# A fourth w_mod row in the last stage, its products on GpSimd, and gradient products and copies in another order

## The chip, the cores and the metric

One core of a Trainium2 chip runs the kernel. The metric is the device time of one execution in microseconds, the median over several runs. A core has five engines with a queue each: TensorE (PE, with its weight loads shown as PEld), VectorE (DVE), ScalarE (ACT), GpSimd (POOL) and SyncE (SP). DMAs are issued from the queues of SP, POOL and ACT.

## What is computed

The forward pass of one transformer-like block and all its gradients: an adaptive layer norm, a spectral filter (2D real FFT, a product with a complex weight, inverse FFT), a second adaptive layer norm and an MLP with GELU. All data is bf16, with 2048 tokens, D = 1024 and F = 3584.

```python
def _A_ref(x, w_r, w_i):
    X = rfft2(x.astype(float32), axes=(-2, -1)) * (w_r + 1j * w_i)
    return irfft2(X, s=(S, D), axes=(-2, -1)).astype(bfloat16)
def _B_ref(x, w1, b1, w2, b2):
    h = gelu(einsum('bsd,df->bsf', layernorm(x), w1) + b1)
    return einsum('bsf,fd->bsd', h, w2) + b2
mod = (silu(c) @ w_mod).reshape(1, 6, 1, -1)
sa, ca, ga, sb, cb, gb = (mod[:, k] for k in range(6))
h = layernorm(A_x) * (1 + ca) + sa
x = A_x + ga * _A_ref(h, A_w_r, A_w_i)
h = layernorm(x) * (1 + cb) + sb
out = x + gb * _B_ref(h, B_w1, B_b1, B_w2, B_b2)
# returned: out, and the gradients for A_x, A_w_r, A_w_i, B_w1, B_b1, B_w2, B_b2, c, w_mod
```

Three of the gradients matter here. The gradient of w_mod (1024 x 6144, out_9) is the outer product of silu(c) and the six gradient rows of mod, each 1024 long. The gradient of c (out_8) needs, for each of those rows, the product of w_mod with that row. The gradients of the MLP weights (out_6 for w2, out_4 for w1) are products over all 2048 tokens.

## The kernel before

The work is a single long program, with no loop left on the chip. The FFTs are matrix products with cosine and sine matrices, split by symmetry into four classes of 512 rows (CE, CO, SE, SO). The part that the change touches is the last third: the backward pass through the spectral filter, beside which the weight gradients of the MLP are computed.

**Filler products.** A generator, `pieces` (L1504), yields one weight gradient product at a time: 16 matmuls of 128x512 into one PSUM buffer, 56 products for out_6 (`gw2_product`) and then 56 for out_4 (L1550). `fill(n)` takes n products from it, so the places of the `fill` calls are where TensorE gets work beside the spectral steps. Four PSUM buffers (`ps_f`) serve the products, and a few of the spectral steps too. ScalarE copies each out_4 product to one of eight buffers in `gwo1` (L1554), and a store from there is issued on POOL's queue, or on SP's for the last three (L1556). The gradient of gelu's input, d_gz, comes in as transposing DMAs on SP (`gw1_load`, L1495), one pair per group of eight products.

**The pair stage.** `spectral_core` runs eight pairs of frequency blocks (`pair`); after each, `beside_bwd` (L1589) takes four products from `fill` and up to three steps of a ring, `gmod_ring` (L1185), that works on rows 3 and 4 of w_mod's gradient: 16 steps, one for each of the eight 128-row blocks of each row. A step reduces a block of w_mod against the gradient row (VectorE, L1201), forms the block of out_9 in the same buffer (VectorE, L1203), stores it (POOL's queue, L1204) and loads the block two steps on (SP's queue, L1190). The ring has three buffers, so a load waits for the store of an earlier step. The loads of the transposed activations for the out_6 products (hhsA, L1507 and L1509) are on SP's queue too.

**The split inverse.** After the pairs, `half_class` (L1422) forms V for the classes CO and SO, with two matmuls of half width, ScalarE evacuations (L807, by the helper `s_copy`) and VectorE sums. One product is filled in behind CO. Then four chunks of output follow (L775), and `consume_bwd` (L1460) finishes each: unfolding on VectorE, the backward pass of the layer norm (`scaled_rows`, `ln_bwd`), a column sum on TensorE (`halves_sum`, L218), and the store of out_1. `ln_bwd` reduces on VectorE (L1244), scales on ScalarE by the result (L1246) and adds on VectorE. In the first chunk and the third, products are filled in between the output blocks, and in all of them behind the store of out_1 and behind the column sum.

**The last stage.** When the chunks are done, rows 5, 2, 1 and 0 of w_mod's gradient follow (`gmod_row`, `gmod_steps`), each with six products behind it, and then the products that are left. A row is broadcast from DRAM into one of two `gr` buffers. Each of its eight steps loads a block of w_mod (SP's queue, L1176, four buffers), forms the block of out_9 in one of four buffers (VectorE, L1177), stores that (POOL's queue, L1178) and reduces on VectorE (L1179). The gradient of c is formed from all the reductions at the end.

**What sets the order.** A planner fixes each engine's order at build time. It takes the program's order as the priority and emits what its own estimates of durations call ready, so a product may come earlier or later than its `fill` call; copies out of PSUM have a raised priority. `issue_after(x)` makes each instruction that is traced in its block, on x's engine, stand behind x in that engine's queue; it is an order and not a wait. At run time each queue is worked off in order, with semaphores between the engines.

Of the kernel before, what the change touches and what calls it, by code (L numbers as in the profile page):

```python
# [13 lines left out]
ACT = mybir.ActivationFunctionType  # L14
ALU = mybir.AluOpType
# [20 lines left out]
def kernel(  # L36
# [24 lines left out]
    nc = tc.nc  # L61
    CE, CO, SE, SO = 0, 1, 2, 3
# [131 lines left out]
    def tt(out, a, b, op):  # L194
        return nc.vector.tensor_tensor(out=out, in0=a, in1=b, op=op)  # L195
# [188 lines left out]
    for j in range(4):  # L384
        for cch in range(NDC):
            pt = ps_f("pt")
            for a in range(4):
                q = (0, 2, 3, 1)[a] if j % 2 == 0 else (1, 3, 2, 0)[a]
# [159 lines left out]
    def spectral_core(fwd, fb, sms, em, css, pt, evac_u, evac_c, evac_v, consume, o4tag, pfs=None, fill=lambda n: None, mid=lambda: None, beside=lambda n, r_in: None):  # L548
# [156 lines left out]
        for par in range(2):  # L705
            for m in range(4):
# [14 lines left out]
                if par == 0 and m > 0:  # L721
# [6 lines left out]
                    else:  # L728
                        cl = (CE, SE)[m - 2]
# [4 lines left out]
        for cl in (CO, SO):  # L734
            if fwd:
                s_inv_half(cl, smis[1], 0)
                continue
            Vs[cl] = reg.tile([P, 8, 512], BF16, name=f"V{cl}", tag=f"uv{cl}")

            def r_cols(c8, i, cl=cl):  # L740
                dc = c8 // 2
                base = (0, 1, 2, 1)[dc] + 256 * (c8 % 2) + (PW if (dc >= 2) == (cl < 2) else 0)
                return R[:, cl * 4 + i, :, :].rearrange("p x w -> p (x w)")[:, base:base + 255:2]

            half_class(cl, Vs[cl], r_cols, evac_v)
            if cl == CO:
                fill(1)
        with tc.issue_after(r_in[0].ins):
            nc.vector.tensor_scalar(out=gm[:, 8:12, :], in0=gm[:, 4:8, :], scalar1=-1.0, scalar2=None, op0=ALU.mult)
        xts = [reg.tile([P, 4, D], BF16, name="xt", tag="sma")[:]]  # L750
# [6 lines left out]
        for i in range(4):  # L757
            if fwd and i == 0:
                tmp, eb, o4 = first
            else:  # L760
                o4, on, tmp = ct[:, 3 * (i % 2)], ct[:, 3 - 3 * (i % 2)], ct[:, 1 + i % 2]
                if fwd and i == 2:
                    eb = tmp
            half = [(cl, eb[:, 2 * k + cl // 2], k * 256 + i // 2 * P) for cl in (CE, SE) for k in range(2)]
            for npp, (cl, ov4, c0) in enumerate((half if i % 2 == 0 else []) + [(cl, o4[:, cl], i * P) for cl in (CO, SO)]):
                if npp in (2, 4):
                    fill(1)
                for hh_ in range(2):
                    npo[0] += 1
                    po = ((ps_d, ps_s) if fwd else (ps_d, ps_s, ps_d, ps_f))[npo[0] % (2 if fwd else 4)]("po")  # L770
                    for d2 in range(2):
                        dc = 2 * hh_ + d2
                        for h in range(2):
                            gi = 2 * dc + h + (4 if (dc >= 2 and cl >= 2) else 0)
                            nc.tensor.matmul(po[:, d2 * 256:(d2 + 1) * 256], lhsT=Vs[cl][:, 2 * dc + h, c0:c0 + P],  # L775
                                             rhs=gm[:, gi, :], start=(h == 0), stop=(h == 1))
                    with tc.high_priority():
                        ov = ov4[:, hh_ * 512:(hh_ + 1) * 512]
                        if fwd or (cl, hh_) != (3, 0):
                            nc.any.tensor_copy(out=ov, in_=po[:])  # L780
                        else:
                            last_po[0] = nc.scalar.copy(out=ov, in_=po[:])
            if i % 2 == 0:
                tt(o4[:, 0:4:2, :], eb[:, 0:2, :], eb[:, 2:4, :], ALU.add)
                if fwd and i == 2:
                    tt(on[:, 0:4:2, :], eb[:, 0:2, :], eb[:, 2:4, :], ALU.subtract)
            elif not fwd or i == 1:
                tt(o4[:, 0:4:2, :], eb[:, 0:2, :], eb[:, 2:4, :], ALU.subtract)
            if i == 0:
                if fwd:  # L790
                    for cl in (CO, SO):
                        s_inv_half(cl, smis[1], 1)
                    ct = reg.tile([P, 4, 4, D], BF16, name="ct", tag=o4tag)
                xts.append(reg.tile([P, 4, D], BF16, name="xt", tag="smb" if fwd else "px0")[:])
            consume(i, o4, tmp, ct[:, 2 - i % 2], xts[i % 2], eb)
# [376 lines left out]
    def gmod_steps(r, wrs, gws, gr):  # L1172
        nc.sync.dma_start(out=gr, in_=d_gmod[r * D:(r + 1) * D].partition_broadcast(P))
        for jc in range(NDC):
            wr, gw = wrs[:, jc % wrs.shape[1], :], gws[:, jc % gws.shape[1], :]
            nc.sync.dma_start(out=wr, in_=w_mod[jc * P:(jc + 1) * P, r * D:(r + 1) * D])  # L1176
            nc.vector.tensor_scalar(out=gw, in0=gr, scalar1=u_rt[:, jc:jc + 1], scalar2=None, op0=ALU.mult)  # L1177
            nc.gpsimd.dma_start(out=out_9[jc * P:(jc + 1) * P, r * D:(r + 1) * D], in_=gw)  # L1178
            nc.vector.tensor_tensor_reduce(out=wr, in0=wr, in1=gr, scale=1.0, scalar=0.0,  # L1179
                                           op0=ALU.mult, op1=ALU.add, accum_out=gu[:, r, jc:jc + 1])  # L1180
            yield
# [57 lines left out]
    def ln_sums(gs):  # L1239
        nc.vector.tensor_scalar(out=gs, in0=gs, scalar1=-1.0 / D, scalar2=None, op0=ALU.mult)  # L1240

    def ln_bwd(g, gsum, n_ap, tmp):
        sc = small.tile([P, 1], FP32, tag="lbsc", bufs=4)
        nc.vector.tensor_tensor_reduce(out=tmp, in0=g, in1=n_ap, scale=-1.0 / D, scalar=0.0,  # L1244
                                       op0=ALU.mult, op1=ALU.add, accum_out=sc[:])
        nc.scalar.activation(out=tmp, in_=n_ap, func=ACT.Identity, scale=sc[:], bias=gsum)  # L1246
        tt(g, g, tmp, ALU.add)

    def scaled_rows(out4, in4, row, gs, r, b):
# [201 lines left out]
    sacc = otl[:, 2 * NT * P:2 * NT * P + D]  # L1451
# [8 lines left out]
    def consume_bwd(i, o4, tmp, tmp2, n1, eb):  # L1460
        if i == 0:
            accCA.append(ps_s("accCA"))
            nc.vector.tensor_copy(out=sacc, in_=eb[:, 0, :])
        elif i == 2:
            tt(sacc, sacc, eb[:, 0, :], ALU.add)
        unfold_d(o4, tmp)
        unfold_tok(o4, tmp)
        load_tok(n1, A_x, i, nc.gpsimd)
        with tc.issue_after(last_po[0].ins):
            norm_act(n1, n1, 0, i)  # L1470
        tt(tmp, o4, n1, ALU.mult)
        s1c = small.tile([P, 4], FP32, tag="s1c")
        scaled_rows(o4, o4, opca_row, s1c, 0, i)
        for q in range(4):
            ln_bwd(o4[:, q, :], s1c[:, q:q + 1], n1[:, q, :], tmp2[:, q, :])
        nc.sync.dma_start(out=n1, in_=chunk_rows(d_gx1, i))
        tt(o4, o4, n1, ALU.add)
        store_tok(out_1, o4, i)
        fill((3, 7, 7, 8)[i])
        halves_sum(accCA[0], tmp, i == 0, i == 3)  # L1480
        fill(1 if i == 2 else 2)
        if i == 3:
            rows = small.tile([P, D], BF16, tag="gmrow", bufs=1)
            store_halves(accCA[0], rows[0:64, 0:KH], tmp, 1)
# [13 lines left out]

    def gmod_row(r, ins):
        with tc.issue_after(ins.ins):  # L1500
            for _ in gmod_steps(r, w1g["wr"], w1g["gw"], w1g["gr"][:, r % 2, :]):
                pass

    def pieces():  # L1504
# [36 lines left out]
        for fg in range(F // 512):  # L1541
            if fg == 3:
                w1g["gz"] += [reg.tile([P, 8, 512], BF16, name=f"gzu{k}", tag=f"uv{k}") for k in range(4)]
            for k in {0: (1,), 1: (2,), 2: (3,), 3: (4, 5, 6)}.get(fg, ()):
                w1g["ins"] = gw1_load(k)
            gz2 = w1g["gz"][2 * w1g["set"][fg]:2 * w1g["set"][fg] + 2]
            for cch in range(NDC):
                acc = ps_f("gw1acc")
                for t in range(NT):
                    nc.tensor.matmul(acc[:], lhsT=n3ns[t // 4][:, t % 4, cch * P:(cch + 1) * P], rhs=gz2[t // 8][:, t % 8, :],  # L1550
                                     start=(t == 0), stop=(t == NT - 1))
                ob = gwo1[:, (fg * NDC + cch) % 8]
                with tc.high_priority():
                    nc.scalar.copy(out=ob, in_=acc[:])  # L1554
                eng = nc.sync if fg == 6 and cch > 4 else nc.gpsimd
                eng.dma_start(out=out_4[cch * P:(cch + 1) * P, fg * 512:(fg + 1) * 512], in_=ob)  # L1556
                yield
# [4 lines left out]
    def fill(n):  # L1562
        for _ in range(n):
            next(todo)
        done[0] += n
# [18 lines left out]
        for step in step_in[3:8]:  # L1584
            behind(step, ins)

    rows34 = gmod_ring((3, 4), gmy, sacc)

    def beside_bwd(n, r_in):  # L1589
        for k in range(4):  # L1590
            fill(1)
            if 3 - k < (2, 3, 3, 3, 3, 3, 0, 0)[n]:
                with tc.issue_after(hh_in[0].ins), tc.issue_after(r_in.ins) if n == 7 else ExitStack():
                    next(rows34)

    spectral_core(False, fbuf2, (smA2, None), em2, [css2[:, 0], css2[:, 1]],
                  new_pair_temps(["t0", "t1", "t2", "t3"]), s_copy, s_copy, s_copy, consume_bwd, "fr", pfs, fill, mid_bwd, beside_bwd)
# [7 lines left out]
    unfold_d(sr[0:1, 0], sr[0:1, 1])  # L1605
    store_gmod([sr[0:1, 0, 0, 0:KH], sr[0:1, 0, 0, KH:D]], 0)

    for r in (5, 2, 1, 0):
        gmod_row(r, w1g["ins"])
        fill(6)  # L1610
    fill(NFC * 4 - done[0])
    fin2 = reg.tile([P, 2, P], BF16, name="fin2", tag="gm")
    make_identity(nc, fin2[:, 0, :])
# [40 lines left out]
```

## Time and profile before

| | us |
|---|---|
| three runs | 1412.69, 1404.64, 1414.53 (median 1412.69) |
| profiled execution | 1412.43 |
| its span | 1410.7 |
| TensorE busy | 1354.3 (96%) |
| VectorE busy | 1066.7 (76%) |
| ScalarE busy | 759.4 (54%) |
| GpSimd busy | 355.4 (25%) |
| mean granted TensorE clock | 0.989 |

Times in the views count from the start of the span, which is 1.7 us shorter than the profiled execution's own time. The stages that the change touches lie in its last 400 us: the pairs from about 1011 to 1154, the split inverse to 1168, the chunks to about 1310 (their vector work reaches to 1325), and the last stage to the end.

Views are quoted as they were given. In a timeline a line has the start, the duration, the engine, the line of the kernel, the operation, what it writes and reads with the shapes, a count where several were merged, and in brackets the idle time before it and what ended that. "SPq" and "ACTq" are instructions that an engine's queue issues without being busy, DMAs above all. A view by windows has, for each engine, busy time and in brackets the number of instructions, then the granted clock of TensorE, the share of time in which the DMA engines were busy, and GB/s. In a view of waits a line has the sum, the number of times and the longest. "min/median/max" are ns.

### The profile page before, as it was taken

What the parts mean: (1) busy time and instruction counts of PE and PEld (TensorE: products, weight loads), DVE (VectorE), ACT (ScalarE), POOL (GpSimd) and SP (SyncE); (2) the same over time, 40 slices, a digit from 0 to 9 for tenths busy, and PEclk for the clock granted to TensorE, in tenths of its full rate; (3) what the DMA queues carried; (4) which work ended last, traced back from release to release, by engine and by line L of the source; (5) the groups of instructions that cost most, each with busy time, mean ns of one, the idle gap of its engine ahead of it and who ended that gap; (6) DMA issues with size and microseconds to landing.
All of it is one profiled execution on the core that took longest, in us unless ns stands there. A gap on an engine that the chain in (4) does not pass through costs nothing. (4 is left out here: it accounts for less than half of the span.)

```text
span 1410.7 us, 18467 instructions
## 1 busy us (share of the span) xinstructions
PE 1354.3 (96%) x6774; PEld 658.6 (47%) x6899; DVE 1066.7 (76%) x1479; ACT 759.4 (54%) x1082; POOL 355.4 (25%) x434
## 2 busy tenths in 40 slices
PE   5898999999999999999999999999999899999998
PEld 2445565444444444444444444444644455444444
DVE  5897889977888787887620678889686778968781
ACT  4775657657967766665314593443622454534311
POOL 5410523201212122112211011011254420322542
PEclk8999999999999999999999999999999999999999
DMA  9972746799787777696999499995499987798993
GB/s 318 282 235 61 199 138 194 253 294 351 255 253 230 235 239 243 192 296 224 287 276 272 119 255 308 257 263 148 123 287 262 262 195 204 218 257 171 282 338 111
DMA packets 360689, 331.12 MB, mean 235 GB/s; under 512 B 207962, under 2 KB 303088, under 8 KB 360470
## 3 DMA queue, kind: packets, MB, share of 16 engines
q1 hardware_dynamic: 319702, 204.96, 55.8%
q0 software_dynamic: 35136, 119.73, 24.1%
q10 hardware_dynamic: 5760, 5.25, 1.2%
q8 instruction: 54, 0.88, 0.3%
q14 instruction: 37, 0.30, 0.1%
HBM read 165.73 MB, written 114.87 MB: 199 GB/s over the span
## 5 line engine op out<-in xcount | busy, mean ns | idle before, releaser
L840 PE MATMUL pp<-gBoT,wt 128*128 128x512 bf16 x874 | 196.5, 380 | 4.3 <-ACT phr L846 1.9
L1131 PE MATMUL pg<-w1T,gzr 128*128 128x512 bf16 x877 | 194.3, 379 | 1.3 <-issue 0.5
L1550 PE MATMUL gw1acc<-gzh,n3n 128*128 128x512 bf16 x627 | 139.1, 379 | 3.8 <-ACT gwo L1554 3.1
L1550 PEld LDWEIGHTS <-n3n 128*128 128x128 bf16 x896 | 87.4, 98 | 108.7 <-issue 5.0
L840 PEld LDWEIGHTS <-wt 128*128 128x128 bf16 x896 | 87.6, 98 | 107.9 <-issue 6.4
L1131 PEld LDWEIGHTS <-gzr 128*128 128x128 bf16 x896 | 86.6, 98 | 108.4 <-issue 5.8
L977 PEld LDWEIGHTS <-w 128*128 128x128 bf16 x896 | 87.2, 98 | 106.9 <-issue 2.5
L977 PE MATMUL pz<-n3Tb,w 128*128 128x512 bf16 x437 | 98.4, 379 | 1.7 <-DVE w2sD L1053 1.0
L977 PE MATMUL pz<-n3Ta,w 128*128 128x512 bf16 x439 | 98.0, 379 | 0.4
L1289 PE MATMUL gw2acc<-gB,hhsA 128*128 128x512 bf16 x405 | 93.1, 384 | 5.1 <-DMA hhsA<-d_hhT 4.5
L195 DVE TENSOR_TENSOR ct<-ct 128x2048 bf16<-128x2048 bf16 (+1 forms) x84 | 91.5, 1117 | 7.6 <-DMA d_n<-ct 3.7
L1031 PEld LDWEIGHTS <-hhA 128*128 128x128 bf16 x608 | 59.0, 98 | 72.8 <-issue 2.6
L980 ACT ACTIVATE gt<-pz,b_col 128x512 bf16<-128x512 f32 x112 | 72.8, 683 | 33.3 <-PE pz L977 33.0
L988 ACT ACTIVATE gt<-gt 128x2048 bf16<-128x2048 bf16 x28 | 53.5, 1911 | 64.5 <-DVE gt L195 64.5
L1554 ACT CAST gwo<-gw1acc 128x512 bf16<-128x512 f32 x56 | 31.9, 582 | 98.5 <-PE gw1acc L1550 70.9
L195 DVE TENSOR_TENSOR gt<-gt,gt 128x2048 bf16<-128x2048 bf16 x56 | 68.5, 1224 | 19.8 <-ACT gt L990 18.5
L1297 ACT CAST gwo<-gw2acc 128x512 bf16<-128x512 f32 x40 | 23.5, 586 | 96.0 <-PE gw2acc L1289 72.7
L1289 PEld LDWEIGHTS <-hhsA 128*128 128x128 bf16 x416 | 40.8, 99 | 53.7 <-DMA hhsA<-d_hhT 5.1
L1556 POOL DMA_DIRECT2D out_dram<-gwo x53 | 29.4, 556 | 107.3 <-ACT gwo L1554 107.0
L1550 PE MATMUL gw1acc<-gzu,n3n 128*128 128x512 bf16 x250 | 55.1, 379 | 0.3
L984 ACT ACTIVATE gt<-gt 128x2048 bf16<-128x2048 bf16 x28 | 53.5, 1910 | 2.3 <-DVE hhC L195 1.6
L990 ACT ACTIVATE gt<-gt 128x2048 bf16<-128x2048 bf16 x28 | 53.4, 1907 | 0.4
(366 smaller groups left out, 2535.8 us busy)
## 6 DMA issues: line engine op xcount, KB each, us to landing
gzr<-d_gz SPq DMA_DIRECT2D x28, 512.0 KB
wblk<-in_w_mod_dram SPq DMA_DIRECT2D x12, 1024.0 KB
out_dram<-otl POOLq DMA_DIRECT2D x48, 256.0 KB, 4.8
d_ph<-pho POOLq DMA_DIRECT2D x21, 512.0 KB, 5.6
d_hh<-hhA POOLq DMA_DIRECT2D x19, 512.0 KB, 5.0
wrw<-in_w_mod_dram SPq DMA_DIRECT2D x32, 256.0 KB
w<-in_B_w_dram SPq DMA_DIRECT2D x7, 1024.0 KB
hhC<-d_ph SPq DMA_DIRECT2D x14, 512.0 KB
```

The costliest lines, as they stand in the source:

```text
L195: return nc.vector.tensor_tensor(out=out, in0=a, in1=b, op=op)
L840: last_pe[0] = nc.tensor.matmul(pp[:], lhsT=wt[:, fc % 4, cch, :], rhs=gBoT[j][:, cch, :], start=(cch == 0), stop=(cch == NDC - 1))
L977: last_pe[0] = nc.tensor.matmul(pz[:], lhsT=w1s[g][:, cch, k * P:(k + 1) * P], rhs=n3T[:, cch, :], start=(cch == 0), stop=(cch == NDC - 1))
L980: z_in = nc.scalar.activation(out=zb[:, k, :], in_=pz[:], func=ACT.Identity, bias=b1_col[:, fc:fc + 1], scale=1.0)
L984: nc.scalar.activation(out=av, in_=zb, func=ACT.Square)
L988: nc.scalar.activation(out=sg, in_=bv, func=ACT.Sigmoid, scale=2.0 * GK)
L990: nc.scalar.activation(out=bv, in_=bv, func=ACT.Sigmoid, scale=-2.0 * GK)
L1031: last_pe[0] = nc.tensor.matmul(pbs[i][:], lhsT=hh[:, k, i * P:(i + 1) * P], rhs=wp[:, k, :], start=False, stop=(g == 6 and k == 3))
L1131: last_pg[0] = nc.tensor.matmul(pgs[i][:], lhsT=gzs[b, g][:, k, i * P:(i + 1) * P], rhs=w1Ts[g][:, k, h * KH:(h + 1) * KH], start=(g == 0 ...
L1289: nc.tensor.matmul(acc[:], lhsT=hh_of(fc)[:, t, :], rhs=gBs[t // 4][:, t % 4, h * KH:(h + 1) * KH], start=(t == 0), stop=(t == NT - 1))
L1550: nc.tensor.matmul(acc[:], lhsT=n3ns[t // 4][:, t % 4, cch * P:(cch + 1) * P], rhs=gz2[t // 8][:, t % 8, :], start=(t == 0), stop=(t == NT ...
L1554: nc.scalar.copy(out=ob, in_=acc[:])
```

## The change

```diff
@@ spectral_core, the split inverse
             half_class(cl, Vs[cl], r_cols, evac_v)
-            if cl == CO:
-                fill(1)
+            fill(1)
@@ spectral_core, the output blocks of a chunk
-                if npp in (2, 4):
+                if npp in (2, 4) and (fwd or (i, npp) != (0, 2)):
                     fill(1)
@@ gmod_steps
-            nc.vector.tensor_scalar(out=gw, in0=gr, scalar1=u_rt[:, jc:jc + 1], scalar2=None, op0=ALU.mult)
+            nc.gpsimd.tensor_scalar(out=gw, in0=gr, scalar1=u_rt[:, jc:jc + 1], scalar2=None, op0=ALU.mult)
@@
-    def ln_bwd(g, gsum, n_ap, tmp):
+    def ln_bwd(g, gsum, n_ap, tmp, order=ExitStack):
...
-        nc.scalar.activation(out=tmp, in_=n_ap, func=ACT.Identity, scale=sc[:], bias=gsum)
+        with order():
+            nc.scalar.activation(out=tmp, in_=n_ap, func=ACT.Identity, scale=sc[:], bias=gsum)
@@ consume_bwd
         tt(tmp, o4, n1, ALU.mult)
+        fill(6 if i else 0)
         s1c = small.tile([P, 4], FP32, tag="s1c")
         scaled_rows(o4, o4, opca_row, s1c, 0, i)
         for q in range(4):
-            ln_bwd(o4[:, q, :], s1c[:, q:q + 1], n1[:, q, :], tmp2[:, q, :])
+            ln_bwd(o4[:, q, :], s1c[:, q:q + 1], n1[:, q, :], tmp2[:, q, :],
+                   (lambda: tc.issue_after(w1g["ev"].ins)) if i else ExitStack)
...
-        fill((3, 7, 7, 8)[i])
+        fill((4, 1, 1, 2)[i])
         halves_sum(accCA[0], tmp, i == 0, i == 3)
-        fill(1 if i == 2 else 2)
+        fill((1, 2, 1, 2)[i])
@@ gmod_row
-            for _ in gmod_steps(r, w1g["wr"], w1g["gw"], w1g["gr"][:, r % 2, :]):
+            for _ in gmod_steps(r, w1g["wr"], w1g["gw"], w1g["gr"][:, (r + (r > 3)) % 2, :]):
@@ pieces
-                    nc.scalar.copy(out=ob, in_=acc[:])
+                    w1g["ev"] = nc.scalar.copy(out=ob, in_=acc[:])
@@ the pair stage
-    rows34 = gmod_ring((3, 4), gmy, sacc)
+    row3 = gmod_ring((3,), gmy, sacc)
...
-            if 3 - k < (2, 3, 3, 3, 3, 3, 0, 0)[n]:
+            if 3 - k < (1, 1, 2, 2, 2, 1, 0, 0)[n]:
...
-                    next(rows34)
+                    next(row3)
@@ the last stage
-    for r in (5, 2, 1, 0):
+    for r in (5, 4, 2, 1, 0):
         gmod_row(r, w1g["ins"])
-        fill(6)
+        fill(5)
```

Row 4 moves from the ring beside the pairs to the last stage, which now has 40 steps instead of 32; the ring keeps the eight steps of row 3, called nine times over six pairs (one call is for the first loads) instead of 17. In the last stage the product that forms a block of out_9 goes from VectorE to GpSimd, whose queue also issues its store. `gr`'s slot is chosen so that neighbouring rows of the new sequence use different ones.

A product is filled in behind the split class SO, and the one between the first chunk's CE and SE output blocks is gone. In chunks 1 to 3, six products come before the layer norm's backward pass instead of behind it, and the ScalarE copies of `ln_bwd` are ordered behind the copy of the sixth of them. The number of products is 112 as before. In the first chunk one more of them stands ahead of the column sum and one less behind it.

## The prediction

> **What bounds the kernel now.** I read the page's totals first, then the chain of waits, the PE's waits in the part that the change touches, and the timelines of PE, ACT and SP around each of them.
>
> ```profile
> span 1410.7 us, 18467 instructions
> PE 1354.3 (96%) x6774; PEld 658.6 (47%) x6899; DVE 1066.7 (76%) x1479; ACT 759.4 (54%) x1082; POOL 355.4 (25%) x434
> ...
> 1307.97 1.11 issue
> 1309.08 0.57 ACT gwo L1554
> ...
> 1309.69 3.61 PE gw1acc L1550 x16
> ...
> 1399.91 7.08 PE gw1acc L1550 x32
> 1406.99 0.03 ACTq L1554
> ```
>
> TensorE works for 96% of the span, and the chain that ends last is, from 1309.69 us on, nothing but gradient products. No matmul is added or removed by the change. So it can gain only what PE stands idle from about 1060 us on, and it loses if anything else finishes later than PE's 1406.99. PE's waits there:
>
> ```profile
> PE gw2acc L1289 <- DMA hhsA<-d_hhT: 4.5, 2, 2.9
> PE gw1acc L1550 <- ACT gwo L1554: 3.1, 2, 1.9
> PE pv L652 <- ACT V L807: 2.9, 1, 2.9
> PE pu L1431 <- ACT smbf L807: 2.0, 3, 0.9
> PE accCA L218 <- DVE ct L195: 1.1, 1, 1.1
> ```
>
> That is 13.6 us. The two waits of 2.9 have a cost beyond their length: in the 20 us around each, the granted clock (before the DMA share) is 0.91 and 0.92, so another 1.8 and 1.6 us go.
>
> ```profile
> 1080.00:1100.00 20.00, 17.08 (x80) 8.01 (x80) 12.56 (x20) 6.25 (x11) 6.46 (x8) 0.91 1.09 264
> 1100.00:1120.00 20.00, 17.10 (x88) 9.40 (x88) 19.97 (x31) 5.86 (x11) 13.26 (x12) 0.92 0.91 269
> ```
>
> **Part 1: row 4 leaves the pair stage.** Eight steps go, each with a load and a store of 256 KB, a reduction and a product on VectorE, and one broadcast load. VectorE's share was off the path. The queue's was not:
>
> ```profile
> SPq L1190 <- DMA out_dram<-otl: 33.1, 9, 9.7
> ...
> 1094.10 0.33 SPq L1190 DMA_DIRECT2D otl<-in_w_mod_dram  x1
> 1094.52 3.06 SPq L1509 DMA_TRANSPOSE hhsA<-d_hh  x1
> ```
>
> SP waits 33.1 us in nine of the ring's loads (L1190) for the ring's own stores, and the hhsA loads that PE needs stand behind them in the same queue. With half of the steps, called one or two per pair, about half of those waits go, and 4 MB of traffic in a stretch where the DMA share is 0.9 to 1.1. I take the 4.5 us of hhsA waits and the 1.8 us of clock as gone: 6.3. The wait at L652 is ACT's, which stood 6.3 us in its queue until a DMA had landed and came late to the evacuations:
>
> ```profile
> 1115.48 0.58 ACT L1297 CAST gwo<-gw2acc 128x512 bf16<-128x512 f32 x1 [6.30 <-DMA otl<-d_hh]
> ```
>
> Less traffic should ease that, but nothing in the change orders it: its 2.9 + 1.6 count half, 2.2. Sum 8.5; bounds 0 (the same waits elsewhere) and 10.8.
>
> **Part 2: a product behind the second split class, one less between the first output blocks.** PE's 2.0 us at L1431 lie inside the second class; the product is placed behind it, so I leave them: 0. In the first chunk one more product now stands before the column sum (L218), some 3.5 us (7.08 for the 32 matmuls of two products, in the chain above), which covers its 1.1 us wait for VectorE: 1.1 gained.
>
> **Part 3: six products early, layer norm copies behind the sixth product's copy.** Two rows of ACT show what this is about:
>
> ```profile
> 1261.99 0.58 ACT L1554 CAST gwo<-gw1acc 128x512 bf16<-128x512 f32 x1 [2.87 <-PE gw1acc L1550]
> 1272.99 2.37 ACT L1246 ACTIVATE ct<-xt,s1c,sc 128x1024 bf16<-128x1024 bf16 x2 [10.42 <-DVE s1c L1240]
> ...
> 1293.44 0.59 ACT L1554 CAST gwo<-gw1acc 128x512 bf16<-128x512 f32 x1 [2.87 <-PE gw1acc L1550]
> 1305.65 3.52 ACT L1246 ACTIVATE ct<-xt,s1c,sc 128x1024 bf16<-128x1024 bf16 x3 [11.63 <-DVE s1c L1240]
> ```
>
> ACT stood 10.4 and 11.6 us at a layer norm copy (L1246) whose scale VectorE had not made, with finished products' copies behind it; four PSUM buffers cover some 14 us of that and no more, hence the 3.1 us of L1550. The added order costs nothing by itself: in both chunks the sixth copy would be free about 3.5 us behind the last quoted copy (1265.5 and 1296.9), long before VectorE's scale (1272.99 and 1305.65). Behind the ordered copies stand VectorE's adds and the out_1 store; neither is later. One product more is out of the way, 3.5 us of cover against waits of at most 1.9: 3.1 gained.
>
> So PE's last product would end 8.5 + 1.1 + 3.1 = 12.7 us earlier, at 1394.3. The span ends 3.7 us behind it now, and the run's own time, 1412.43, is 1.7 above its span: 1399.7 if PE alone decides. (The median shown is 1412.69; 1412.43 is as good as equal.)
>
> **Part 4: five rows at the end, products on GpSimd.** That the slots of gr alternate over five rows instead of four costs nothing, since neighbouring rows still differ. Before:
>
> ```profile
> L1177 DVE TENSOR_SCALAR otl<-gr,u_rt x32: 469/481/553, 1315.2 to 1378.5; 128x1024 bf16<-128x1024 bf16 x32
> L1179 DVE CUSTOM_DVE_ANT_0 wrw<-wrw,gr x32: 1204/1211/1226, 1316.4 to 1378.9; 128x1024 bf16<-128x1024 bf16 x32
> L1178 POOL DMA_DIRECT2D out_dram<-otl x32 | 17.5, 547 | 30.9 <-DVE otl L1177 30.7 <-issue 0.2
> out_dram<-otl POOLq DMA_DIRECT2D x48, 256.0 KB, 4.8
> ```
>
> 32 steps run from 1315.2 to 1378.9, 28 us before PE's end; at that 1.99 us a step, 40 would take 80 and still hide. But the product moves from a 0.48 us instruction to an engine that shows no such product. The nearest rows:
>
> ```profile
> L419 POOL TENSOR_SCALAR gidx<-genv x20: 472/692/1795, 16.7 to 56.1; 128x512 int32<-128x512 f32 x12, 128x256 int32<-128x256 f32 x8
> L419 POOL TENSOR_SCALAR gidx<-genv 128x512 int32<-128x512 f32 x12 | 8.6, 719 | 15.5 <-ACT smB L447 14.7
> L419 POOL TENSOR_SCALAR gidx<-genv 128x256 int32<-128x256 f32 x8 | 7.1, 895 | 1.7 <-ACT smB L447 1.2
> ...
> 49.68 2.29 DVE L195 TENSOR_TENSOR fbuf<-fbuf,rows 128x4096 bf16<-128x4096 bf16 x1
> 50.51 1.79 POOL L419 TENSOR_SCALAR gidx<-genv 128x256 int32<-128x256 f32 x1 [1.21 <-ACT smB L447]
> ```
>
> From 0.472 (256 elements, the shortest) to 0.719 (512) is 0.965 ns an element, so 1024 cost 0.719 + 0.494 = 1.21 us; bounds 0.48 (VectorE's own) and 3.6 (four times the 256 group's mean). That mean is so high because of the last two rows: the GpSimd instruction ran into a VectorE instruction with two inputs in SBUF and ended 0.33 us behind it (52.30 against 51.97), where alone it takes 0.47. So the two exclude each other but for 0.14 us. The reduction of L1179 has two such inputs, wr and gr. A longer case, with the reductions back to back, is an indirect store:
>
> ```profile
> 1316.44 1.22 DVE L1179 CUSTOM_DVE_ANT_0 wrw<-wrw,gr 128x1024 bf16<-128x1024 bf16 x1
> 1317.59 0.08 DVE L1179 DVE_READ_ACCUMULATOR2_ANT gu<- 128x1 f32 x1
> ...
> 1325.82 5.58 POOL L167 DMA_INDIRECT out_dram<-ct,xu  x1 [2.24 <-DVE ct L195]
> ```
>
> Its other executions begin at 1.01 us. The Trainium skill, "SBUF — State Buffer", section "Who interferes with whom", says that such a VectorE instruction and a GpSimd instruction that reads SBUF fully block each other; the quoted rows agree. The skill's "GPSIMD Engine Reference", section 4.1, sends elementwise work to VectorE but calls a one-input instruction on GpSimd roughly line-rate; that speaks for the low end of my 1.21.
>
> Now the sum. Reductions: 40 at a pitch of 1.15 (1317.59 less 1316.44) = 46.0. Products: 40 x (1.21 - 0.14) = 42.8. Chunk 3's last adds on VectorE and its two indirect stores, by their rows about 2.3 + 1.3 + 1.3 and 2 x 1.0:
>
> ```profile
> 1323.27 2.27 DVE L195 TENSOR_TENSOR ct<-ct,xt 128x4096 bf16<-128x4096 bf16 x1
> 1330.84 1.27 DVE L195 TENSOR_TENSOR sr<-sr 1x512 f32<-1x512 f32 x2
> 1333.19 1.28 DVE L195 TENSOR_TENSOR sr<-sr 1x512 f32<-1x512 f32 x2
> ```
>
> That is 95.7 us of a resource that one of the two holds at a time; GpSimd's 0.55 us DMA issues lie beside the reductions. It starts with the first row's broadcast, 1315.2 less the gains ahead of it (8.5 + 1.1, and the 1.2 of chunk 2) = 1304.4. So the last product ends at 1400.1, its store lands 0.55 + 4.8 later at 1405.5, 7 us behind PE's own end. With 1.7 around it 1407.2, and one us for gradient stores still queued on POOL: **1408 us**. The gain ahead is real, and the new tail gives most of it back.
>
> **Rivals.** *The tail stays under PE* (24%). VectorE's reductions wait for loads often enough that GpSimd's products fall into gaps, or cost nearer 0.48. Then PE decides: 1396 to 1402, about 1400. For it: 28 us of slack before. Against: 88.8 us for products and reductions alone, in some 90 from the first row to PE's end.
>
> *POOL's queue starves PE* (20%, the slower side). Gradient stores (L1556) stand in POOL's queue among the row stores in an order fixed at build time:
>
> ```profile
> 1377.94 0.59 ACT L1554 CAST gwo<-gw1acc 128x512 bf16<-128x512 f32 x1 [3.88 <-DMA out_dram<-gwo]
> 1379.27 0.54 POOL L1178 DMA_DIRECT2D out_dram<-otl  x1 [1.19 <-DVE otl L1177]
> 1379.80 4.79 POOL L1556 DMA_DIRECT2D out_dram<-gwo  x9
> ```
>
> Already before, nine such stores were left behind the last row store, and ACT's copies waited for a free one of the eight gwo buffers; only PSUM kept PE going. If a step costs 2.42 (1.21 + 1.21, no overlap) and more, or VectorE keeps GpSimd out as at 1325.82, the same order puts the store that frees PE's last buffers at about 40 x 2.5 = 100 us, and another 4.8 to land, two or three products and the end: 1304 + 100 + 5 + 9 + 4 + 1.7 = 1424. At 2.7 us a step 1432. It decides from about 2.5 us on. I put it at 1428.
>
> *The upstream gain doesn't come* (8%): hhsA waits for the remaining ring's stores, and the tail hides or nearly so: 1411 to 1418.
>
> **Chances and range.** Forecast 48% (1402 to 1416). For 8 in 10 the range reaches from the first rival to the start of the second: 1396 to 1426. About 1% of 1412.7, 14 us, is what a measurement of this kernel can tell from no change. Faster than 1398.6 needs PE-bound and nearly all waits gone: 14% of the 24, and 2 of the rest: 0.16. Slower than 1426.8: most of the POOL rival and a little beside: 0.18. Within: 0.66.
>
> **What would show it.** Right: no hhsA wait above 1 us and a granted clock of 1.00 around 1090; ACT with no 10 us wait at L1246 ahead of a sixth product's copy; GpSimd products of 1.2 us alone and above 2 next to L1179; the last row store, not a matmul, near the end of the span. Wrong: products under 0.7 us, or rows done 10 us before PE (then about 1400); PE waiting at L1550 for gwo copies in the last 90 us (then above 1420).

## The result, and the profile after

The changed kernel takes 1471.86 us (median of six runs, 1468.03 to 1478.97) against 1411.43 for the kernel before: a ratio of 1.0445, with an interval of 1.0408 to 1.0482. The forecast was 1408 with a range to 1426. The profiled execution took 1478.97, its span is 1477.2, and its mean granted clock 0.970.

From the page of the changed kernel, the totals, the chain that ended last, and ScalarE's copies of the gradient products (busy time and mean ns after the first bar, the idle time before them and its releaser after the second):

```profile
PE 1368.2 (93%) x6773; PEld 660.1 (45%) x6899; DVE 1063.8 (72%) x1440; ACT 758.8 (51%) x1081; POOL 473.3 (32%) x474
POOL 8%; PE 2%; issue 2%; DVE 1%; DMA 1%; SPq 0%; POOLq 0%
L1556 ACT CAST gwo<-gw1acc 128x512 bf16<-128x512 f32 x56 | 32.1, 582 | 178.6 <-DMA out_dram<-gwo 133.2
```

TensorE still has the largest share of busy time, but the chain that ends last runs through GpSimd. The product that the change put there, seen by itself (min, median and max in ns, first and last start), and all that POOL did from the first of these products to the last row store, grouped:

```profile
L1176 POOL TENSOR_SCALAR otl<-gr,u_rt x40: 2834/2852/5554, 1301.7 to 1461.7; 128x1024 bf16<-128x1024 bf16 x40
```

```profile
L1176 POOL TENSOR_SCALAR otl<-gr,u_rt 128x1024 bf16<-128x1024 bf16 x40 | 126.5, 3169 | 13.4 <-DMA gr<-d_gmod 12.7
L1177 POOL DMA_DIRECT2D out_dram<-otl x40 | 22.2, 556 | 0.0
L1558 POOL DMA_DIRECT2D out_dram<-gwo x22 | 12.7, 578 | 0.0
L167 POOL DMA_INDIRECT out_dram<-ct,xu x2 | 2.9, 1435 | 0.6 <-DVE gu L1178 0.3 <-issue 0.3
```

The product takes 3.17 us on average where the prediction took 1.21. The four sums make 164.3 us, and from 1301.7 to the end of the last row store at 1466.2 there are 164.5: POOL works without a pause, one instruction behind the other, products and DMA issues alike. The idle 12.7 lies ahead of the first product. So a step costs 4.1 us in all, and what else stands in POOL's queue waits. TensorE's waits in the part that the change touches (sum, times, longest), then a stretch of POOL's timeline and the two matmul runs beside it:

```profile
PE gw1acc L1552 <- ACT gwo L1556: 42.9, 14, 6.9
PE accCA L218 <- DVE ct L195: 3.0, 1, 3.0
```

```profile
1407.46 9.05 POOL L1176 TENSOR_SCALAR otl<-gr,u_rt 128x1024 bf16<-128x1024 bf16 x2
1416.47 0.59 POOL L1558 DMA_DIRECT2D out_dram<-gwo  x1
1417.06 1.09 POOL L1177 DMA_DIRECT2D out_dram<-otl  x2
1418.18 5.67 POOL L1176 TENSOR_SCALAR otl<-gr,u_rt 128x1024 bf16<-128x1024 bf16 x2
1423.81 0.59 POOL L1558 DMA_DIRECT2D out_dram<-gwo  x1
```

```profile
1409.33 3.61 PE L1552 MATMUL gw1acc<-gzh,n3n 128*128 128x512 bf16 x16 [1.38 <-ACT gwo L1556]
1419.25 5.48 PE L1552 MATMUL gw1acc<-gzh,n3n 128*128 128x512 bf16 x16 [6.30 <-ACT gwo L1556]
```

The planner put one gradient store (L1558) behind about every two row products. The store frees a `gwo` buffer, ScalarE's copy needs that buffer, TensorE needs the PSUM that the copy empties: ScalarE's copies wait 133.2 us for such stores, and TensorE 42.9 us for the copies. A product of 16 matmuls takes 3.61 us at full clock and 5.48 behind the wait of 6.30; the granted clock (the third figure from the end) falls in the tail:

```profile
1080.00:1100.00 20.00, 19.89 (x101) 9.80 (x101) 14.82 (x20) 5.38 (x9) 7.57 (x9) 1.00 1.02 249
1346.00:1380.00 34.00, 19.45 (x69) 7.80 (x70) 17.50 (x27) 2.34 (x4) 33.85 (x23) 0.83 0.55 188
1420.00:1477.00 57.00, 23.02 (x78) 8.92 (x78) 0.28 (x1) 4.69 (x8) 49.15 (x39) 0.71 0.26 97
```

The first of these windows is the one in the pair stage where the clock was 0.91 before. Ahead of the last stage the change did most of what it was predicted to do. TensorE's waits at hhsA and L652 and, up to there, for `gwo` copies are gone, and so are those at L1431, which the prediction had left in place. The wait at the column sum (accCA, above), counted as gone, is 3.0 us in this trace where it was 1.1. The ring's wait on SP's queue, which was 33.1 us and of which the prediction took about half as gone, is gone as a whole:

```profile
SPq L1189 <- DMA out_dram<-otl: 0.3, 1, 0.3
```

The column sums of the last chunk (the matmuls into accSA) start at 1313.1 in the trace before and at 1301.8 after, with as many gradient products done, and the changed kernel's profiled run is 2.2 us late at 940 us, ahead of all that the change touches: some 13.5 us were gained up to there, and more than 70 lost behind it.

### The profile page after: what moved, and what is told of

Read it like the earlier page. It is cut to its first block, busy times and chain, and to the rows that moved or that the text cites. A ratio compares the mean times of both kernels' runs of the same rounds, so it can differ in the third digit from the quotient of the medians.

```text
span 1477.2 us, 18421 instructions
## 1 busy us (share of the span) xinstructions
PE 1368.2 (93%) x6773; PEld 660.1 (45%) x6899; DVE 1063.8 (72%) x1440; ACT 758.8 (51%) x1081; POOL 473.3 (32%) x474
## 5 line engine op out<-in xcount | busy, mean ns | idle before, releaser
L1552 PE MATMUL gw1acc<-gzh,n3n 128*128 128x512 bf16 x625 | 150.0, 398 | 25.4 <-ACT gwo L1556 24.7
L1552 PEld LDWEIGHTS <-n3n 128*128 128x128 bf16 x896 | 90.9, 102 | 162.5 <-issue 68.8
L1176 POOL TENSOR_SCALAR otl<-gr,u_rt 128x1024 bf16<-128x1024 bf16 x40 | 126.5, 3169 | 13.4 <-DMA gr<-d_gmod 12.7
L1556 ACT CAST gwo<-gw1acc 128x512 bf16<-128x512 f32 x56 | 32.1, 582 | 178.6 <-DMA out_dram<-gwo 133.2
L1178 DVE CUSTOM_DVE_ANT_0 wrw<-wrw,gr 128x1024 bf16<-128x1024 bf16 x40 | 56.3, 1451 | 52.8 <-DMA wrw<-in_w_mod_dram 36.7
L987 ACT ACTIVATE gt<-gt 128x2048 bf16<-128x2048 bf16 x28 | 53.5, 1910 | 64.5 <-DVE gt L195 64.5
L1552 PE MATMUL gw1acc<-gzu,n3n 128*128 128x512 bf16 x251 | 60.9, 402 | 18.6 <-ACT gwo L1556 18.2
L1558 POOL DMA_DIRECT2D out_dram<-gwo x53 | 29.9, 566 | 80.2 <-ACT gwo L1556 80.2
```

The lines of the kernel that those rows point to most:

```text
L987: nc.scalar.activation(out=sg, in_=bv, func=ACT.Sigmoid, scale=2.0 * GK)
L1176: nc.gpsimd.tensor_scalar(out=gw, in0=gr, scalar1=u_rt[:, jc:jc + 1], scalar2=None, op0=ALU.mult)
```

## The experiments

Four batches, each with its own runs of the kernel before (medians 1407.48, 1410.38, 1408.27 and 1410.45).

**Products back on VectorE, the rest of the change kept.**

```diff
-            nc.gpsimd.tensor_scalar(out=gw, in0=gr, scalar1=u_rt[:, jc:jc + 1], scalar2=None, op0=ALU.mult)
+            nc.vector.tensor_scalar(out=gw, in0=gr, scalar1=u_rt[:, jc:jc + 1], scalar2=None, op0=ALU.mult)
```

> The changed kernel with the last stage's products back on VectorE; all else as changed. Theory (the GpSimd product, 2.85 us in the changed kernel's trace instead of the 1.21 of the prediction, is the whole loss; the rest of the change brings what its sum said): the 40 steps go at about 2.0 us each and end before TensorE, no wait of TensorE at the gradient products in the last 90 us above 1 us, time 1397 to 1403. Rival (five rows are too much for the last stage on any engine, by traffic or by queue): above 1420, with TensorE waiting for gwo copies.

Measured: 1394.05 us, ratio 0.9916 (0.9886 to 0.9946), 3 us below the expected band. This version beats both kernels. Its product group, and the only wait over 1 us that TensorE has left in this part:

```profile
L1176 DVE TENSOR_SCALAR otl<-gr,u_rt x40: 467/480/556, 1293.9 to 1364.7; 128x1024 bf16<-128x1024 bf16 x40
PE pu L1431 <- ACT smbf L806: 2.4, 3, 1.7
```

Forty steps take 71 us and end 24 us before TensorE's last product. The engine of that one instruction makes 78 us by the medians (75 by the ratios, each against its own runs of the kernel before), the whole loss. The wait at the column sum does not appear here.

**GpSimd products alone, in the kernel before.** The same line changed the other way; four rows, 32 products.

> The kernel before with only the engine of the last stage's products changed to GpSimd: four rows, 32 products, the old fills. Theory: a step costs what it costs in the changed kernel, (1465.6 - 1301.7) / 40 = 4.1 us, so 32 take 131 us from 1315 on, 1446, and the time is about 1450 to 1457. Rival (the fifth row, or the new order of products, is what makes POOL's queue late): below 1425.

Measured: 1459.23 us, ratio 1.0381 (1.0341 to 1.0422), 2 us above the expected band.

```profile
L1177 POOL TENSOR_SCALAR otl<-gr,u_rt x32: 2832/2849/5306, 1312.0 to 1438.5; 128x1024 bf16<-128x1024 bf16 x32
PE gw1acc L1550 <- ACT gwo L1554: 38.2, 13, 6.9
```

The same price and the same wait for gradient copies without anything else of the change: the loss needs neither the fifth row nor the moved products.

**What makes the instruction slow: two sets of probes.** Both add instructions to the kernel before, behind POOL's last store, where nothing else runs; `prb` is bf16, `prf` f32. The kernels' own times contain the probes and are not read. The first varies type, size and scalar of the one-operation form, the second repeats it with a second operation that changes nothing.

```diff
+    with tc.issue_after(w1g["st"].ins):
...
+                nc.gpsimd.tensor_scalar(out=dst[:, 1, 0:n], in0=src[:, 0, 0:n], scalar1=s, scalar2=None, op0=ALU.mult)
```

> The kernel before with single GpSimd instructions behind the last store on POOL, on scratch data, while VectorE is nearly idle: a product by a scalar with 1024 elements a partition from bf16 to bf16, f32 to bf16, bf16 to f32 and f32 to f32, with 512 from bf16 to bf16 and f32 to f32, with a constant in place of the scalar operand, and a copy from bf16 to bf16. If bf16 is what makes it slow: f32 to f32 at 1024 about 1.2 us (0.965 ns an element as in the rows of the page), bf16 to bf16 2.85, the two mixed forms tell whether reading or writing costs it. If the size or the plain one-operation form is: f32 to f32 is 2.85 too. If the scalar operand is: the constant form is near 1.2. The added instructions lengthen the end of the run; its time says nothing.

```diff
+                nc.gpsimd.tensor_scalar(out=dst[:, 1, 0:n], in0=src[:, 0, 0:n], scalar1=s, scalar2=s2, op0=ALU.mult, op1=o1)
...
+            nc.gpsimd.tensor_tensor(out=pb[:, 1, :], in0=pb[:, 0, :], in1=pb[:, 0, :], op=ALU.mult)
```

> The probes of before with two operations: times a scalar operand, plus 0.0, from bf16 to bf16 and f32 to f32 at 1024 elements and from bf16 to bf16 at 512; times a constant plus 0.0; times a scalar operand times 1.0, f32; and a plain product of two bf16 tensors at 1024. If the second operation is the difference: 1024 elements about 1.2 us, 512 about 0.72, in either type. If something else of the page's rows is (their integer output, or that their input is an f32 ramp): 2.83 and 1.55 as with one operation. The added instructions lengthen the end of the run; its time says nothing.

The first set:

```profile
L1635 POOL TENSOR_SCALAR prb<-prb,u_rt 128x1024 bf16<-128x1024 bf16 x3 | 8.5, 2844 | 0.0
L1635 POOL TENSOR_SCALAR prf<-prf,u_rt 128x1024 f32<-128x1024 f32 x3 | 8.5, 2832 | 0.0
L1635 POOL TENSOR_SCALAR prb<-prb,u_rt 128x512 bf16<-128x512 bf16 x3 | 4.7, 1552 | 0.0
L1637 POOL COPY prb<-prb 128x1024 bf16<-128x1024 bf16 x3 | 3.1, 1037 | 0.2
```

And the second:

```profile
L1635 POOL TENSOR_SCALAR prb<-prb,u_rt 128x1024 bf16<-128x1024 bf16 x3 | 3.4, 1117 | 0.0
L1635 POOL TENSOR_SCALAR prf<-prf,u_rt 128x1024 f32<-128x1024 f32 x6 | 6.7, 1114 | 0.0
L1635 POOL TENSOR_SCALAR prb<-prb,u_rt 128x512 bf16<-128x512 bf16 x3 | 2.1, 685 | 0.0
L1637 POOL TENSOR_TENSOR prb<-prb 128x1024 bf16<-128x1024 bf16 x3 | 5.7, 1894 | 0.2
```

The type makes no difference. The number of operations does: 2.84 us with one, 1.12 with two, on the same 1024 elements, and 1.55 against 0.69 on 512. The instructions of L419, from which the prediction took its price, all have two (a multiplication and an addition), and their 0.72 us for 512 elements agrees with the 0.69 here. Why one operation costs more than two, no run shows.

**The product with a second operation.** The changed kernel with a cheap form of the same product.

```diff
-            nc.gpsimd.tensor_scalar(out=gw, in0=gr, scalar1=u_rt[:, jc:jc + 1], scalar2=None, op0=ALU.mult)
+            nc.gpsimd.tensor_scalar(out=gw, in0=gr, scalar1=u_rt[:, jc:jc + 1], scalar2=0.0, op0=ALU.mult, op1=ALU.add)
```

> The changed kernel with the same GpSimd products written as two operations (times the scalar, plus 0.0), like the 128x512 rows of 0.72 us in the page, where all probes with one operation took 1.55. The computed values are the same. Theory 1 (the one-operation form is what costs 2.83 us; the rest of the prediction stands): a product takes 1.2 us alone and about 2 beside a reduction with two inputs, the rows take 40 x 2.2 to 2.4 us, 88 to 96, and end with TensorE or a little behind it: 1394 to 1412. Theory 2 (1024 elements or bf16 on GpSimd cost 2.8 us in any form): nothing changes, about 1465.

Measured: 1421.08 us, ratio 1.0068 (1.0046 to 1.0091). 51 us of the loss are gone with the form of the instruction alone, but the time is above the expected band. POOL from 1297.9 on, grouped as above, and TensorE's wait:

```profile
L1176 POOL TENSOR_SCALAR otl<-gr,u_rt 128x1024 bf16<-128x1024 bf16 x40 | 71.3, 1790 | 15.5 <-DMA gr<-d_gmod 13.3 <-DMA out_dram<-otl 1.4
L1177 POOL DMA_DIRECT2D out_dram<-otl x40 | 22.0, 552 | 0.0
L1558 POOL DMA_DIRECT2D out_dram<-gwo x22 | 12.5, 567 | 0.0
L167 POOL DMA_INDIRECT out_dram<-ct,xu x2 | 3.8, 1884 | 0.6 <-issue 0.3 <-DVE gu L1178 0.3
```

```profile
PE gw1acc L1552 <- ACT gwo L1556: 10.6, 7, 2.2
```

109.6 us of work in the 111.1 from 1298.0 to 1409.1, again without a gap to speak of: 2.7 us a step. The products have a median of 1.13 but a mean of 1.79: by the timelines, 22 of the 40 run beside VectorE instructions with two inputs and take 2.34 us on average, the other 18 take 1.12. The longest case has two products beside three reductions and the end of a fourth:

```profile
1318.91 6.40 POOL L1176 TENSOR_SCALAR otl<-gr,u_rt 128x1024 bf16<-128x1024 bf16 x2
```

The 34.5 us of DMA issues add to the products.

**The same without the reductions.** The reductions of the last stage become a copy of one element, so their part of the gradient of c is not computed.

```diff
-            nc.vector.tensor_tensor_reduce(out=wr, in0=wr, in1=gr, scale=1.0, scalar=0.0,
-                                           op0=ALU.mult, op1=ALU.add, accum_out=gu[:, r, jc:jc + 1])
+            nc.vector.tensor_copy(out=gu[:, r, jc:jc + 1], in_=wr[:, 0:1])
```

> e6 (two-operation products on GpSimd, 1.12 us alone, 1.79 in the mean) with the last stage's 40 reductions replaced by a one-element copy each, which keeps the waits for the loads; the gradient of c is not computed from those rows. Theory (beside the reductions with two SBUF inputs the products wait, 40 x 0.67 = 27 us): the products take 1.1 to 1.2 us each, POOL's stream shrinks to 40 x (1.12 + 0.55) + 13 + 4 = 84 us, TensorE decides again: 1390 to 1399. Rival (the products are slow there for another reason, as the load of the DMA queues): the mean stays above 1.6 us and the time above 1412.

Measured: 1395.14 us, ratio 0.9911 (0.9892 to 0.9931).

```profile
L1176 POOL TENSOR_SCALAR otl<-gr,u_rt x40: 1112/1127/1877, 1298.6 to 1383.6; 128x1024 bf16<-128x1024 bf16 x40
```

The mean is 1141 ns here, so with the reductions there a product takes 0.65 us longer on average over all 40, 26 us in all. Without them POOL is done in time and TensorE decides again.

**The DMA issues out of POOL's queue: three tries.** First the gradient stores on ScalarE's queue, with the product of the change and with the two-operation product:

```diff
-                eng = nc.sync if fg == 6 and cch > 4 else nc.gpsimd
+                eng = nc.sync if fg == 6 and cch > 4 else nc.scalar
```

> The changed kernel (one-operation products on GpSimd) with the out_4 gradient stores issued from ScalarE's queue instead of POOL's. Theory (POOL's own serial work sets the end, TensorE's waits are only its echo through the gwo buffers): TensorE has no wait for gwo copies and its last product ends near 1392; POOL still does 40 x (3.17 + 0.55) and two indirect stores, 153 us from 1302 on, so the time is 1455 to 1464. Rival (TensorE's starvation through POOL's queue is what lengthens the run): 1395 to 1415.

> e6 with the out_4 gradient stores issued from ScalarE's queue instead of POOL's; all reductions in place. Theory (POOL is a serial stream of waits, products and issues): 40 x (1.79 + 0.55) and two indirect stores, 97 us from 1298 on, then the last store: 1398 to 1405, and TensorE without waits for gwo copies. Rival (the shared port alone paces the rows, as the prediction had it, and the issues lie beside it): within 4 us of e6's 1421.

Measured: 1458.32 us, ratio 1.0354 (1.0311 to 1.0397), and 1430.34, ratio 1.0155 (1.0113 to 1.0197). TensorE's and ScalarE's waits in the second of them:

```profile
PE gw1acc L1552 <- ACT gwo L1556: 27.4, 4, 10.0
ACT gwo L1556 <- DMA wrw<-in_w_mod_dram: 42.6, 7, 12.3
ACT gwo L1556 <- DMA gr<-d_gmod: 24.0, 3, 18.0
```

The first lies in the expected band and the second does not. In both TensorE was to run free, and waited 52.4 and 27.4 us. Its copies stand behind stores in ScalarE's queue that, by the releasers in the profile, are issued only when loads of the last stage, from SP's queue, have come (`wrw`, `gr`), data that a gradient store doesn't need. Why they are tied together stays open. The first run does bear on what the issues cost, since POOL sets its end as expected:

```profile
L1176 POOL TENSOR_SCALAR otl<-gr,u_rt 128x1024 bf16<-128x1024 bf16 x40 | 127.8, 3201 | 22.1 <-DMA gr<-d_gmod 21.5
```

From the first product at 1296.0 to the end of the last row store at 1451.4 POOL needs 155.4 us, 9.1 less than the 164.5 of the changed kernel, with 12.7 us of issues gone and some 3 us of gaps added; TensorE's last product ends before that, at 1447.3. In the second run POOL is done at 1403.7 and TensorE, starved through ScalarE's queue, sets the end.

With the two-operation product, the row stores were then put on SP's queue instead:

```diff
-            nc.gpsimd.dma_start(out=out_9[jc * P:(jc + 1) * P, r * D:(r + 1) * D], in_=gw)
+            nc.sync.dma_start(out=out_9[jc * P:(jc + 1) * P, r * D:(r + 1) * D], in_=gw)
```

> The two-operation products on GpSimd again, and the last stage's stores of out_9 issued on SP's queue instead of POOL's. If POOL is one serial stream (products 71.3 us, row stores' issues 22.0, gradient stores' issues 12.5, two indirect stores 3.8 in the run with the stores on POOL, together 109.6 of the 111.1 us that its rows took), 22 us leave it: the stream is 88 us and ends at 1386 to 1398 (the upper end if each of the five rows waits some 2 us for its broadcast), TensorE waits under 2 us for gradient copies, and the time is 1394 to 1404. If the issues lie beside the reductions, as the prediction counted them, and only the products and their waits for the shared port set the pace, taking the issues away changes nothing: 1416 to 1424. Below that a third way is possible: SP's queue holds loads behind stores that wait for products; then POOL shows waits for its row buffers or for the broadcast row of more than 10 us, and the time lies between.

Measured: 1416.53 us, ratio 1.006 (1.0038 to 1.0083): the third way, though the time lies just above what it allowed. POOL's groups from 1295 on, and two places of SP's and POOL's timelines at the change from one row to the next:

```profile
L1176 POOL TENSOR_SCALAR otl<-gr,u_rt 128x1024 bf16<-128x1024 bf16 x39 | 71.2, 1834 | 21.8 <-DMA wrw<-in_w_mod_dram 10.8 <-issue 10.4
```

```profile
1335.51 0.33 SPq L1177 DMA_DIRECT2D out_dram<-otl  x1
1335.89 0.42 SPq L1172 DMA_DIRECT2D gr<-d_gmod  x1
```

```profile
1341.35 9.42 POOL L1176 TENSOR_SCALAR otl<-gr,u_rt 128x1024 bf16<-128x1024 bf16 x4 [4.78 <-issue]
```

SP issues the broadcast of the next row (L1172) only behind the row's last store, which waits for the last product; POOL then has nothing to do until the row has come, 4.7 to 6.2 us at each of four changes. The 22 us of issues came back as 21 us of waits (10.8 and 10.4 by their releasers). That the issues add to the products is shown by the gapless sums of POOL's groups; the run with the gradient stores on ScalarE's queue and the product of the change is 13.5 us faster than the changed kernel without 12.7 us of them, though it changes ScalarE's queue too. With the two-operation product, that the time falls when the issues alone go, no run shows.

**Products on ScalarE.** `nc.scalar.activation(out=gw, in_=gr, func=ACT.Identity, scale=...)` in place of the GpSimd product.

> The changed kernel with the last stage's products on ScalarE, which is the least busy engine there (15 us of 70 in the kernel before). Theory: about 1.2 us each, 40 x 1.2 = 48 us beside 28 copies of 0.58; the products stand in the same queue as the copies that free TensorE's buffers, so some waits of TensorE are possible, but the time is 1397 to 1406. Rival (five rows too much on any engine): above 1420.

Measured: 1416.24 us, ratio 1.0068 (1.0043 to 1.0093).

```profile
ACT otl L1176 <- DMA out_dram<-otl: 17.3, 19, 4.4
PE gw1acc L1552 <- ACT gwo L1556: 15.0, 7, 5.5
```

The products are cheap, 1.15 us, and done by 1366, but each may wait for its row buffer, and the gradient copies stand behind it in ScalarE's queue. The expectation counted ScalarE's spare time and not its order.

**The upstream parts.** Row 4 moved alone in the kernel before, with its calls of the ring and its `gr` slots as in the change, but VectorE products; and the moved products and ordered copies alone, with the rows and the ring as before and VectorE products:

```diff
-    rows34 = gmod_ring((3, 4), gmy, sacc)
+    row3 = gmod_ring((3,), gmy, sacc)
...
-    for r in (5, 2, 1, 0):
+    for r in (5, 4, 2, 1, 0):
         gmod_row(r, w1g["ins"])
-        fill(6)
+        fill(5)
```

> The kernel before with part 1 alone: row 4 leaves the ring beside the pairs and joins the last stage, with VectorE products, and five fills a row there; no other edit. By the prediction's sum: no hhsA wait of TensorE above 1 us, no stretch of half clock near 1090 and perhaps one near 1118, 6.3 to 10.8 us less than before. Rival (the waits come elsewhere, or the new order of products does it): less than 3 us.

> The kernel before with parts 2 and 3 alone: the moved products and the layer norm copies behind the sixth product's copy; rows 3 and 4 in the ring and four rows at the end, VectorE products as before. By the prediction's sum: the waits of TensorE at the gradient products for gwo copies (3.1 us) and at the column sum (1.1) go, those of the pair stage stay: 4.2 us less than before. Rival (the pair stage also profits, or the order costs as much as it brings): under 2 or above 7.

Measured: 1398.98 us, ratio 0.9910 (0.9890 to 0.9929), and 1402.88, ratio 0.9948 (0.9930 to 0.9966), against 1410.38: gains of 11.4 and 7.5 us. The first gain is just above the expected 6.3 to 10.8; the second lies in the band of its rival, above 7, by which the pair stage also profits. TensorE's waits over 1 us, of the first and of the second:

```profile
PE gw1acc L1550 <- ACT gwo L1554: 3.7, 2, 1.9
```

```profile
PE gw2acc L1289 <- DMA hhsA<-d_hhT: 3.1, 1, 3.1
PE pv L652 <- ACT V L806: 1.5, 1, 1.5
```

Each part takes away its own waits, hhsA in the first and the `gwo` copies in the second, and both shorten those at L652 and L1431 as well. So the two don't add up: 11.4 and 7.5, and 13.4 together. By the intervals of the ratios, row 4 alone gains 10 to 16 us and all parts together 8 to 16, so it is not shown that the moved products add anything to it.

## Why the prediction was wrong

**The step that failed** is the price in part 4: "so 1024 cost 0.719 + 0.494 = 1.21 us". The product takes 2.84 us alone, as the probes and the minimum of its group show, and 3.17 on average. The rows of L419 were the right engine and the right opcode with another form of the instruction. The bounds, 0.48 and 3.6, held the true value, but the range didn't carry the upper one through to the time: it stopped at 1426, 18 us above the forecast, which is a product of 1.21 + 18 / 40 = 1.66 us. By the prediction's own sum, 2.84 in the place of 1.21 gives 46.0 + 40 x (2.84 - 0.14) + 6.9 = 160.9 us from 1304.4, and with the same ends behind it 1473. The measured median is 1471.86. So it is a term that was mis-sized, in a sum whose shape served, if partly by luck: in the trace POOL's work starts 2.7 us earlier and takes 3.6 us more than this sum has it, and the next two points are errors that nearly cancel.

**"GpSimd's 0.55 us DMA issues lie beside the reductions"** was wrong too. They lie in POOL's own queue, behind the products: 34.9 us of 164.3 in the changed kernel.

**The reductions were charged in full.** The prediction let each product and each reduction exclude the other but for 0.14 us, and so counted all 46.0 us of reductions. In the changed kernel the products lose 3.17 - 2.85 = 0.32 us each and the reductions 1.45 - 1.21 = 0.24. These are means over all 40: 17 products run beside VectorE instructions with two inputs and take 3.61 us on average, the other 23 take 2.85. One pair of products with the reductions beside it, from the timelines of POOL and VectorE:

```profile
1348.70 6.81 POOL L1176 TENSOR_SCALAR otl<-gr,u_rt 128x1024 bf16<-128x1024 bf16 x2
```

```profile
1348.38 1.22 DVE L1178 CUSTOM_DVE_ANT_0 wrw<-wrw,gr 128x1024 bf16<-128x1024 bf16 x1
1349.53 2.13 DVE L1178 CUSTOM_DVE_ANT_0 wrw<-wrw,gr 128x1024 bf16<-128x1024 bf16 x1
1351.59 1.21 DVE L1178 CUSTOM_DVE_ANT_0 wrw<-wrw,gr 128x1024 bf16<-128x1024 bf16 x1
1353.34 1.52 DVE L1178 CUSTOM_DVE_ANT_0 wrw<-wrw,gr 128x1024 bf16<-128x1024 bf16 x1 [0.53 <-DMA wrw<-in_w_mod_dram]
1354.79 1.21 DVE L1178 CUSTOM_DVE_ANT_0 wrw<-wrw,gr 128x1024 bf16<-128x1024 bf16 x1
```

Between 1348.70 and 1355.51 two products (5.7 us alone) and the larger part of five reductions pass, some 10.7 us of work in 6.81. So this product and a reduction wait for each other, but not for all of their length. From 1328 on, where the reductions are VectorE's only instructions there with two large inputs, products and reductions lie side by side for 31.1 us, and together they are 14.8 us longer than alone (at 2.85 and 1.21), about half. With the two-operation product it is 26.0 of 29.5 us: for the instruction that the prediction had priced, its 0.14 us was nearly right. The Trainium skill, "SBUF — State Buffer", section "Who interferes with whom", calls the port that the two share an exclusive lock; the two-operation product nearly agrees with that, the one-operation product does not.

What the sum had wrong is that POOL is not always beside a reduction, and has issues besides. The two errors work against each other: the reductions' 46 us, counted in full, stood where 34.9 us of issues and 12.8 us of waiting products belonged. With the cheap product they no longer cancel: the rule gives 40 x (1.12 - 0.14) + 46.0 + 6.9 = 92.1 us, and POOL took 109.6, of which 26 are the products' waiting and 34.5 the issues.

**The rival that came true** is "POOL's queue starves PE", with its mechanism (gradient stores among row stores in a fixed order, copies without a buffer, TensorE without PSUM) and the sign named for it, TensorE waiting for `gwo` copies. It had 20% and 1428, since it was priced from steps of 2.5 to 2.7 us, and the step is 4.1. At 2.7 us, as the two-operation product has it, it gave 1432 where 1421 was measured. The Trainium skill, "GPSIMD Engine Reference", section 4.1, was quoted as speaking for a cheap product, with one-input work on GpSimd roughly at line rate. For this form the runs show 2.84 us, beside 0.48 on VectorE and 1.15 on ScalarE; its other advice, elementwise work on VectorE, is what the best version does.

**Parts 1 to 3 held.** Predicted 12.7 us and 1399.7 if TensorE decides, on a profiled execution of 1412.4; with the products on VectorE the gain is 13.4, and the trace of the changed kernel shows 13.5 up to the last stage, where the sum had 10.8 (8.5 + 1.1 + 1.2). The hhsA waits went and the clock is 1.00 where it was 0.91. ScalarE still stands up to 12.0 us at a layer norm copy (L1246), but TensorE no longer waits for `gwo` copies ahead of the last stage. The division was less good: row 4 alone gives 11.4 against 8.5, the other parts 7.5 against 4.2, because waits that either part removes (L652, and L1431, which was left at its 2.0) were credited by half, or not at all. That the total agrees is in part luck.

## What to carry to other kernels

Price an added instruction by a row of the same form, the number of operations and operands included, and if there is none, carry both bounds through to the time. An engine that is to take on work is a queue: add up everything in it from the first instruction to the last, DMA issues with it, and ask which of them frees a buffer that the bounding engine needs. Moving an instruction to an engine with idle time gained nothing on GpSimd or ScalarE here, since in both the stores or copies that keep TensorE going stood behind it.

## What the runs showed of the hardware

- A `tensor_scalar` on GpSimd with one operation takes 2.3 to 2.5 times as long as with two: 2.84 and 1.12 us for 128x1024, in bf16 and f32 alike, 1.55 and 0.69 for 128x512 in bf16; a copy of 128x1024 takes 1.04.
- GpSimd products and two-input VectorE reductions delay each other. Of the time that they lie side by side, 26.0 of 29.5 us are lost with the product of 1.12 us, and 14.8 of 31.1 with that of 2.85.
- In GpSimd's queue a DMA issue of some 0.55 us adds to the compute instructions: 34.9 us of 164.3 in the changed kernel.
